# The first mixer group: where its residual comes from

## The chip, the cores and the metric

The kernel runs on one NeuronCore of a Trainium2 chip. It uses TensorE (PE; its weight loads are shown apart as PEld), VectorE (DVE), ScalarE (ACT), GpSimd (POOL) and SyncE (SP), which issues transfers. The metric is the device time of one launch in microseconds (us); lower is better. Times of whole runs are medians; all times inside the kernel come from one profiled execution, counted from the start of its span.

## The reference

Eight batches, eight heads, 576 tokens, head width 64. First an attention with a causal mask and a bias from a running sum, then a mixer: a low-rank product along the sequence (rank 32) and an MLP along the channels, both with a residual. The heads side by side make the 512 features of `x`.

```python
def _attn_ref(q, k, v, s):
    ...
    scores = scale * np.matmul(q, k.transpose(0, 1, 3, 2))
    cum = np.cumsum(np.maximum(s, 0.0), axis=-1)
    bias = -(cum[:, :, :, None] - cum[:, :, None, :])
    scores = np.where(causal, -1000000000.0, scores + np.minimum(bias, 0.0))
    ...
    return np.matmul(attn, v).astype(np.float32)

def _moe_ref(x, U, V, w_ch1, w_ch2):
    xt = x.transpose(0, 2, 1)
    h = xt @ U @ V
    u = x + h.transpose(0, 2, 1)
    ch = np.maximum(u @ w_ch1, 0.0) @ w_ch2
    return (u + ch).astype(np.float32)
```

`U` is 576x32, `V` 32x576, `w_ch1` 512x2048, `w_ch2` 2048x512. What matters below is the last line: the result is the sum of `u` and of the second channel product, and `u` itself is `x` plus the sequence mixer's part.

## The kernel before, in words

**Stages.** The attention works on pairs of heads (32 pairs, four to a batch): `transposes(n)` turns q and k on PE and copies them into a `slot` (lines 303, 323, 326), `scores(n)` makes scores and exponentials (lines 391, 409, 421, 427), `values(n)` multiplies by V (line 455), and DVE divides (line 465) into `x_sb`, a tile of `[token in tile, pair, token tile, feature]`, that is, `x` in token order. `x_sb` is allocated once to a batch from a ring of two.

**The mixer's groups.** The 4608 tokens (8 x 576) are cut into nine groups of 512. A group's `uT` holds `u` with features on the partitions, as the first channel product needs it. For batch 0, `mix_first` makes it: it multiplies `x_sb` by `U_sb` into `ux_first` (line 572; `U_sb` has 128 columns of which 32 are not zero, so rows 32 to 127 of `ux_first` are zero), turns `x_sb` on PE and adds `ux_first` times `V_sb` into the same PSUM tile (lines 579, 587). `mix_first_end` does the last 64 tokens (lines 602, 610). Group 0 is the first 512 tokens of batch 0.

**The channel MLP of a group** is `chanmix(g)`. `hidden` (line 624) makes 16 blocks `hT` with a ReLU on ACT (line 992; the first four of group 0 at line 1135). Group 0 then makes its result by `outputs`: for each of four 128-token tiles `i`, 16 matmuls of 512 columns add up in one PSUM tile (line 634). The first halves of tiles 0 and 1 are made ahead. Line 1017 adds the residual on DVE, line 1023 sends 256 KB. Groups 1 to 8 use `outputs_by_quarters` (line 673) instead, a scheme with fewer products.

**The residual** must be in token order. `by_token` (line 979) fetches it with a transposing transfer from `uT` into `u_sd`, issued on SP; groups 0 to 6 share one `u_sd` buffer. SP also issues the row loads of the slots (line 289), the transposing transfers of `x_sb` to `xT` from batch 2 on (line 472) and the outputs.

**Order.** The text's order is woven: `chanmix` and others are generators in a list `fill`, and attention steps are interleaved with `step_fill()` at a pace; each `yield` is one portion. On PE and POOL the text's order is kept to the end of the kernel (`in_program_order`, line 1263). On DVE, ACT and SP it is kept only up to line 1148, the end of the opening; after that the order on these three is chosen at compile time by the framework's scheduler from its estimates. PSUM tiles for all this (`pwork`) come from a ring of four banks. Between the opening and group 0's outputs, lines 1187 and 1188 copy `V_sb`'s 32 rows to partitions 32 to 127 and into `V_end`, which later batches use.

Of the kernel before, what the change touches and what calls it, by code (L numbers as in the profile page):

```python
# [39 lines left out]
def kernel(  # L40
# [12 lines left out]
    nc = tc.nc  # L53
# [15 lines left out]
    NF = FF // 128  # L69
# [14 lines left out]
    def pwork():  # L84
        return ps_w.tile([128, 512], FP32, tag="w", name="pwork")
# [65 lines left out]
    V_sb = consts.tile([128, S], BF16)  # L151
# [116 lines left out]
    uT_of, x_of, xT_of = {}, {}, {}  # L268

    def uT(g):  # L270
        if g not in uT_of:
            uT_of[g] = work.tile([128, 4, 512], BF16, tag="uT", name="uT", bufs=3)
        return uT_of[g]
# [292 lines left out]
    ux_first = work.tile([128, PB, 128], BF16, tag="ux_first", name="ux_first", bufs=1)  # L566
# [29 lines left out]
        yield  # L596

    def mix_first_end():
        x_sb = x_of.pop(0)
        ut = pwork()[:, 0:256].rearrange("p (a b) -> p a b", a=4)  # L600
        for dt in range(4):
            nc.tensor.matmul(
                ut[:, dt, :],
                lhsT=x_sb[:, dt, 4, :],
                rhs=identity[:, :64],
                start=True,
                stop=False,
                skip_group_check=True,
            )
            nc.tensor.matmul(  # L610
                ut[:, dt, :],
                lhsT=ux_first[:, dt, :],
                rhs=V_sb[:, 512:S],
                start=False,
                stop=True,
                skip_group_check=True,
            )
        nc.vector.tensor_copy(uT(1)[:, 0:4, 0:64], ut)
# [3 lines left out]
    def hidden(f1, u, nf, kts):  # L622
        for kt in kts:
            nc.tensor.matmul(  # L624
                f1,
                lhsT=w1_sb[:, kt, ds(nf * 128, 128)],
                rhs=u[:, kt, :],
                start=(kt == 0),
                stop=(kt == 3),
            )  # L630

    def outputs(f2, hT, i, nfs):
        for nf in nfs:
            nc.tensor.matmul(  # L634
                f2,
                lhsT=hT[:, nf, ds(i * 128, 128)],
                rhs=w2_sb[:, nf, :],
                start=(nf == 0),
                stop=(nf == NF - 1),
                skip_group_check=True,  # L640
            )
            if nf % 4 == 3 and nf < nfs[-1]:
                yield
# [9 lines left out]
    def first_sums(hT, one):  # L653
        if one:
            total(A_1, hT[:, :HF, 256:], hT[:, HF:, 256:], ALU.add, 0)
        else:
            total(A_2, A_1, hT[:, :HF, :256], ALU.subtract, 0)
# [313 lines left out]
    def by_token(u, late=False):  # L971
        if late:
            x_sb = work.tile([128, PB, 5, 128], BF16, tag="x_sb", name="x_sb")
            u_sd = x_sb.rearrange("p a b c -> p (a b c)")[:, 0:2048].rearrange(
                "p (a b c) -> p a b c", a=4, b=4
            )
        else:
            u_sd = work.tile([128, 4, 4, 128], BF16, tag="u_sd", name="u_sd", bufs=1)
        nc.sync.dma_start_transpose(
            out=u_sd.rearrange("p a b c -> p (a b) c"), in_=u.rearrange("p a b -> p (a b)")  # L980
        )
        return u_sd

    def chanmix(g, hT=None, done=0):
        u = uT_of.pop(g)
        if g > 0:
            hT = work.tile([128, NF, 512], BF16, tag="hT", name="hT")
            sums = {1: weight_sums, NG - 3: first_weight_sums}.get(g, lambda: iter(()))()
        for nf in range(done, NF):
            f1 = pwork()  # L990
            hidden(f1, u, nf, range(4))
            nc.scalar.activation(hT[:, nf, :], f1, RELU)  # L992
            if g > 0:
                next(sums, None)
            if g > 0 and nf in (12, 14):
                first_sums(hT, nf == 12)
            if nf == (3 if g > 0 else NF - 1):
                u_sd = by_token(u)
            if nf == NF - 1:
                expanded.append(g)  # L1000
            yield
        if g > 0:
            yield from outputs_by_quarters(g, hT, u_sd)
            return
        ahead = {}
        if g == 0:
            for i in range(2):
                ahead[i] = pwork()
                for _ in outputs(ahead[i], hT, i, range(8)):
                    yield  # L1010
                yield
        for i in range(4):
            f2 = ahead[i] if i in ahead else pwork()
            for _ in outputs(f2, hT, i, range(8 if i in ahead else 0, NF)):
                yield
            o_sb = work.tile([128, DM], FP32, tag="o_sb", name="o_sb", bufs=3)
            nc.vector.tensor_tensor(
                o_sb.rearrange("p (a b) -> p a b", a=4),
                f2.rearrange("p (a b) -> p a b", a=4),
                u_sd[:, :, i, :],  # L1020
                op=ALU.add,
            )
            nc.sync.dma_start(out=out_flat[ds(g * 512 + i * 128, 128), :], in_=o_sb)
            yield
# [120 lines left out]
    hidden_first(2)  # L1145
    hidden_first(3)
    mix_first_end()
    in_program_order(tc, traced, [E.DVE, E.Activation, E.SP])
    load_v(1)
# [7 lines left out]
    load(2)  # L1157
    load_v(2)
    fill.append(chanmix(0, first_hT, 4))
    pace[1] = 0  # L1160
    made = {}
# [29 lines left out]
    weave("V4 V4 S7 V5 S7 V5 S7 V6 S7 V6 T8 T8 V7 S8 V7 S8 T9 S8 T9")  # L1191
    weave("S8 S9 M1 S9 M1 S9 M1 M1 S9 M1 F M1")
    fill.append(chanmix(1))
    pace[1] = 11
    for n in range(2 * PB, NP + 2):
        b, hp = divmod(n, PB)
        if hp == 0 and b < B - 1:
            load(b + 1)
        mixing = seqmix(b - 1) if hp == 1 and b > FT else iter(())
        if b == B:  # L1200
            fill_with(3)
            for _ in range(3):
                step(mixing)
                fill_with(2)
        if n > 2 * PB and n + 1 < NP:
            for at, _ in enumerate(transposes(n + 1)):
                step_fill()
                if at == 0:
                    step(mixing)
        if 2 * PB + 1 < n < NP:  # L1210
            for at, _ in enumerate(scores(n, pT_of(n))):
                step_fill()
                if at == 1:
                    step(mixing)
        for _ in mixing:
            fill_with(1)
        if hp == 1 and FT < b < B:
            fill.append(chanmix(b - 1))
            pace[1] = 12 if b < 6 else 10
        if 2 * PB < n <= NP:  # L1220
            run(values(n - 1, pT_of(n - 1)))
        if hp == 0 and 2 <= b < B - 1:
            load_v(b + 1)
# [20 lines left out]
    for g, sets, fills in ((NG - 2, 4, (0, 0, 2, 4, 6, 8, 10, 12, 14, 17, 20, 23, 25, 26)), (NG - 1, 4, (1, 3, 5, 7, 9, 11, 13, 16, 19, 22, 25, 25, 26, 26))):  # L1244
        u = uT_of.pop(g)
        u_sd = by_token(u, True)
        hT = work.tile([128, NF, 512], BF16, tag="hT", name="hT")
# [46 lines left out]
```

## Time and profile before

| | us |
|---|---|
| median of 3 runs | 361.93 (361.89 to 363.06) |
| profiled execution | 360.82 |
| its span | 359.1 |
| granted PE clock | 1.00 |
| DVE busy in the span | 275.0 |
| ACT busy in the span | 212.8 |
| line 634, first and last start | 48.3, 74.2 |
| line 1017 (four adds), first and last start | 58.4, 74.7 |
| u_sd transfers issued on SP (seven), first and last | 30.9, 277.8 |

The span runs from the first to the last instruction of the program; the execution's own time is 1.7 us longer. Busy time of an engine counts its instructions, not its waits. A matmul's row includes the time to drain, which overlaps with the next, so the step from one matmul's start to the next is what it costs in a stream. Some matmul records are missing: 58 of line 634's 64 are there, while all 64 weight loads are.

### The profile page before, as it was taken

How to read it: one execution, taken by the hardware profiler on the slowest of the kernel's cores; microseconds unless marked ns; L12 is line 12 of the kernel's file. 1: busy time of each engine (PE TensorE's matmuls, PEld its weight loads, DVE VectorE, ACT ScalarE, POOL GpSimd, SP SyncE). 2: the span in 40 equal slices, each digit the busy share in tenths (PEclk: the TensorE clock that was granted, in tenths of full speed). 3: DMA queues.
4: the chain of work that ended last, by engine and by line, in shares of the span. 5: the costliest groups of instructions: out<-in, count | busy, mean ns of one | idle time of the engine just before them, and what ended most of it. 6: DMA issues, size and time to landing. Idle time of an engine off the chain costs nothing.

```text
span 359.1 us, 9577 instructions
## 1 busy us (share of the span) xinstructions
PE 348.8 (97%) x3983; PEld 256.5 (71%) x4022; DVE 275.0 (77%) x608; ACT 212.8 (59%) x322; POOL 84.1 (23%) x102
## 2 busy tenths in 40 slices
PE   8999999999999999999999999999899999999996
PEld 4685566666688567876688667876588548888885
DVE  8685777698889758985799568985797779676774
ACT  4786966757760787157833785358742554675710
POOL 8897261714040404040404022000000000000000
PEclk9999999999999999999999999999999999999999
DMA  7999999999998997999996999172033515010022
GB/s 106 156 200 202 160 178 141 164 160 133 107 112 108 158 133 61 72 120 134 109 94 73 126 149 82 50 162 46 0 49 74 130 36 113 29 60 31 30 89 88
DMA packets 158243, 37.94 MB, mean 106 GB/s; under 512 B 142840, under 2 KB 156568, under 8 KB 158200
## 3 DMA queue, kind: packets, MB, share of 16 engines
q0 software_dynamic: 113136, 18.50, 83.2%
q1 hardware_dynamic: 44776, 18.64, 30.4%
q8 instruction: 31, 0.51, 0.6%
q10 hardware_dynamic: 288, 0.20, 0.2%
q14 instruction: 12, 0.10, 0.1%
HBM read 37.25 MB, written 9.70 MB: 131 GB/s over the span
## 4 chain that ended last, share of the span: by engine, by line
PE 78%; DVE 11%; ACT 4%; DMA 3%; issue 3%; DVEq 0%; ACTq 0%; POOLq 0%
PE pwork L624 22%; PE pwork L673 12%; PE quarter L673 10%; PE pscore L391 8%; PE pwork L455 7%; PE parts L903 6%; PE pwork L303 4%; PE pwork L634 3%; DMA xT<-x_sb 2%; DVE uT L509 2%; DVE slot L651 2%; DVE slot L326 2%; ACT pT L409 2%; ACT hT L992 2%; PE pscore L352 1%
## 5 line engine op out<-in xcount | busy, mean ns | idle before, releaser
L624 PE MATMUL pwork<-uT,w_sb 128*128 128x512 bf16 x401 | 105.9, 379 | 2.6 <-ACT hT L992 0.9
L992 ACT ACTIVATE hT<-pwork 128x512 bf16<-128x512 f32 x108 | 65.2, 608 | 38.4 <-PE pwork L624 38.2
L409 ACT ACTIVATE pT<-pscore 128x1024 bf16<-128x1024 f32 x56 | 56.4, 1030 | 48.7 <-PE pscore L391 47.9
L624 PEld LDWEIGHTS <-w_sb 128*128 128x128 bf16 x448 | 38.3, 98 | 35.9 <-issue 1.3
L391 PE MATMUL pscore<-slot 68*128 68x320 bf16 (+1 forms) x500 | 55.4, 246 | 0.6 <-ACT hT L409 0.3
L391 PEld LDWEIGHTS <-slot 68*128 68x128 bf16 x564 | 41.4, 97 | 16.5 <-issue 0.9
L169 POOL DMA_DIRECT2D v_slot<-in_v_dram x40 | 33.9, 865 | 77.0 <-PE pwork L455 66.3
L673 PEld LDWEIGHTS <-hT 128*128 128x128 bf16 x496 | 46.3, 98 | 7.0 <-DVE uT L509 0.5
L335 DVE TENSOR_TENSOR pT<-pT,keep 128x512 bf16<-128x512 bf16 (+1 forms) x81 | 28.6, 354 | 21.8 <-ACT pT L409 15.9
L323 DVE COPY slot<-pwork 64x576 bf16<-64x576 bf16 x76 | 34.4, 453 | 4.6 <-PE pwork L303 3.7
L455 PEld LDWEIGHTS <-pT 128*128 128x128 bf16 x870 | 32.5, 98 | 6.7 <-issue 1.5
L455 PE MATMUL pwork<-v_slot,pT 128*128 128x65 bf16 x870 | 35.9, 193 | 0.5 <-DVE uT L509 0.4
L465 DVE TENSOR_TENSOR x_sb<-pwork,rec 128x320 bf16<-128x320 f32 x64 | 31.2, 489 | 1.4
L421 ACT ACTIVATE pT<-pscore 128x1024 bf16<-128x1024 f32 x29 | 30.3, 1044 | 2.6 <-PE pscore L391 2.4
L673 PE MATMUL pwork<-w_sb,hT 128*128 128x256 bf16 x240 | 30.6, 273 | 0.0
L326 DVE COPY slot<-pwork 64x576 bf16<-64x576 bf16 x30 | 24.1, 802 | 6.7 <-PE pwork L303 6.2
L673 PEld LDWEIGHTS <-slot 128*128 128x128 bf16 x256 | 24.1, 98 | 4.6 <-issue 1.6
L113 POOL DMA_DIRECT2D q_sd<-in_q_dram x6 | 12.6, 2108 | 45.0 <-PE pwork L303 33.7
L464 DVE RECIPROCAL rec<-pwork 128x5 f32<-128x5 f32 x64 | 12.1, 190 | 12.3 <-PE pwork L455 11.9
L673 PE MATMUL pwork<-w_sum,slot 128*128 128x256 bf16 x160 | 20.3, 273 | 0.7 <-DVE o_sb L687 0.7
L303 PEld LDWEIGHTS <-q_sd 72*128 72x128 bf16 x256 | 14.8, 99 | 8.6 <-DMA q_sd<-in_q_dram 1.0
L303 PE MATMUL pwork<-identity,q_sd 72*128 72x72 bf16 x256 | 18.2, 198 | 0.1
(162 smaller groups left out, 537.1 us busy)
## 6 DMA issues: line engine op xcount, KB each, us to landing
out_dram<-o_sb SPq DMA_DIRECT2D x34, 256.0 KB
v_slot<-in_v_dram POOLq DMA_DIRECT2D x32, 128.0 KB, 7.5
w_sb<-in_moe_w_ch_dram POOLq DMA_DIRECT2D x4, 1024.0 KB, 13.6
q_sd<-in_q_dram POOLq DMA_DIRECT2D x5, 576.0 KB, 13.5
k_sd<-in_k_dram POOLq DMA_DIRECT2D x5, 576.0 KB, 21.9
q_sd<-in_q_dram POOLq DMA_DIRECT2D x4, 288.0 KB, 13.0
k_sd<-in_k_dram POOLq DMA_DIRECT2D x4, 288.0 KB, 12.5
q_sd<-in_q_dram POOLq DMA_DIRECT2D x4, 144.0 KB, 4.9
```

The lines of the kernel that those rows point to most:

```text
L169: nc.gpsimd.dma_start(out=vt[:rows_t, t, :, 0:D], in_=v[b, :, ds(t * 128, rows_t), :].rearrange("h p d -> p h d"),)
L303: nc.tensor.transpose(tps[hh][:, c, t2, :], src[:, 2 * hp + hh, ds(t2 * 128, 128)], identity[:TP, :TP],)
L323: copies(n, hh, par)(by_run[:, :, :, par, :], src)
L326: copies(n, hh, par)(in_turn[:, :, :, :, par], src.rearrange("p c t m -> p c m t"))
L391: nc.tensor.matmul(dst, lhsT=slot[0:KA, hh, ds(S + j * 128, 128)], rhs=slot[0:KA, hh, lo:hi], start=True, stop=True,)
L409: nc.scalar.activation(pT[:, hh, 0:1024], near, EXP, scale=scale)
L421: nc.scalar.activation(pT[:, :, 1024:1536], mid.rearrange("p (a b) -> p a b", a=2), EXP, scale=scale)
L455: nc.tensor.matmul(po[:, i, :], lhsT=pT[:, hh, ds(place(j, i), 128)], rhs=vt[:, j, h, :], start=(j == 0), stop=(j == i), skip_group_check= ...
L465: nc.vector.tensor_tensor(x_sb[:, hp, :, ds(hh * D, D)], po[:, :, 0:D], rec.to_broadcast([128, 5, D]), op=ALU.mult,)
L624: nc.tensor.matmul(f1, lhsT=w1_sb[:, kt, ds(nf * 128, 128)], rhs=u[:, kt, :], start=(kt == 0), stop=(kt == 3),)
L673: nc.tensor.matmul(acc[:, i, :], lhsT=a[:, kt, ds(i * 128, 128)], rhs=b[:, kt, :], start=(begin and i == 0 and kt == 0), stop=(kt == HF - ...
L992: nc.scalar.activation(hT[:, nf, :], f1, RELU)
```

## The change

Group 0 no longer fetches `u` back in token order. Its residual is put together from two parts: `x` itself, which is there in token order as `x_sb`, is added by DVE at the end, and the sequence mixer's part is made by one more matmul at the head of each tile's accumulation, `V_sb`'s 128 columns of the tile as weights and `ux_first` (128x512) as the moving operand. So the PSUM tile holds `h` plus the channel product, and the add brings `x`. The transposing transfer of group 0 is not issued. `x_sb` of batch 0 is kept (`x_of[0]` is read, not popped, in `mix_first_end`) until `chanmix(0)` has used it. The other groups are as before, except that group 1 is now the first user of the `u_sd` buffer.

```diff
     def mix_first_end():
-        x_sb = x_of.pop(0)
+        x_sb = x_of[0]
...
     def outputs(f2, hT, i, nfs):
         for nf in nfs:
+            if nf == 0:
+                nc.tensor.matmul(
+                    f2,
+                    lhsT=V_sb[:, ds(i * 128, 128)],
+                    rhs=ux_first.rearrange("p a b -> p (a b)"),
+                    start=True,
+                    stop=False,
+                    skip_group_check=True,
+                )
             nc.tensor.matmul(
                 f2,
                 lhsT=hT[:, nf, ds(i * 128, 128)],
                 rhs=w2_sb[:, nf, :],
-                start=(nf == 0),
+                start=False,
                 stop=(nf == NF - 1),
                 skip_group_check=True,
             )
...
-            if nf == (3 if g > 0 else NF - 1):
+            if g > 0 and nf == 3:
                 u_sd = by_token(u)
...
+        x_sb = x_of.pop(0)
         ahead = {}
-        if g == 0:
-            for i in range(2):
-                ahead[i] = pwork()
-                for _ in outputs(ahead[i], hT, i, range(8)):
-                    yield
+        for i in range(2):
+            ahead[i] = pwork()
+            for _ in outputs(ahead[i], hT, i, range(8)):
                 yield
+            yield
...
                 o_sb.rearrange("p (a b) -> p a b", a=4),
                 f2.rearrange("p (a b) -> p a b", a=4),
-                u_sd[:, :, i, :],
+                x_sb[:, :, i, :],
                 op=ALU.add,
```

The line `if g == 0` that goes away was always true at that place.

## The prediction

> **What bounds the kernel now.** I read the engine totals first, then the list of what TensorE (PE) waited for, then the rows and the order of time around the group that changes. The totals:
>
> ```profile
> span 359.1 us, 9577 instructions
> PE 348.8 (97%) x3983; PEld 256.5 (71%) x4022; DVE 275.0 (77%) x608; ACT 212.8 (59%) x322; POOL 84.1 (23%) x102
> ```
>
> PE has work for 97% of the span, and the chain that ended last lies on it for 78%. All PE waits of over a tenth that the waits view lists add up to 4.9 us, 1.3 of them before the first matmul. So the first question to any edit here is what it adds to PE or takes from it; the second is whether one of the few waits changes. The rows of the first group's last product (line 634) and of its transfer:
>
> ```profile
> L634 PEld LDWEIGHTS <-hT x64: 95/96/102, 48.3 to 74.0; 128*128 128x128 bf16 x64
> L634 PE MATMUL pwork<-w_sb,hT x58: 376/378/383, 48.4 to 74.2; 128*128 128x512 bf16 x58
> ```
>
> and SP's order of time:
>
> ```profile
> 30.95 7.65 SPq L979 DMA_TRANSPOSE u_sd<-uT  x1
> 46.27 12.08 SPq L289 DMA_DIRECT2D slot<-rows_hbm  x6
> ...
> 75.38 0.35 SPq L1023 DMA_DIRECT2D out_dram<-o_sb  x1
> ```
>
> The reader should see three things: the 64 matmuls (58 recorded) run from 48.4 to 74.2 us, woven between attention work; the transfer that goes away was issued at 30.95; SP then had nothing to issue until 46.27. The first add that reads what the transfer brought (line 1017) starts at 58.4. Nobody waits for it: the view of the tile u_sd names no waiter.
>
> **What is added.** Four matmuls, one at the head of each 128-token tile, of the form 128x512 with 128x128 weights, the form of line 634. The 378 ns of a row includes the time to drain, so the price in a stream is read from the chain, where the next matmul starts:
>
> ```profile
> 68.19 0.86 PE pwork L634 x4
> 69.06 0.06 PE pwork L497
> 69.11 0.44 PE pscore L391 x4
> 69.55 0.86 PE pwork L634 x4
> ```
>
> Here 0.86 us for four gives 0.215 us each, and their weight loads of 96 ns run under the matmul before. So 4 x 0.215 = 0.86 us of PE. The trace does not show this operand pair. Lower bound 0.215 each; upper bound a matmul that overlaps with nothing, 0.378 + 0.096 = 0.474, or 1.90 us for four. I take 0.215, because in that chain a stretch of four takes 0.86 to 0.87 also where its first matmul opens a tile (69.55). The granted clock in all stretches is 1.00.
>
> The Trainium skill, "TensorE: Matmul & The Clock Gate", section "Back-to-back issue gap", puts a sustained stream of weight load and matmul at about 131 ns for 512 columns. By that estimate the four would cost 0.52 us; the row says 0.86, and the row is used.
>
> Do all four lengthen the path? The second tile's opening waits:
>
> ```profile
> 51.13 0.81 DVE L326 COPY slot<-pwork 64x576 bf16<-64x576 bf16 x1
> ...
> 51.63 0.10 PEld L634 LDWEIGHTS <-hT 128*128 128x128 bf16 x1
> ...
> 51.99 0.38 PE L634 MATMUL pwork<-w_sb,hT 128*128 128x512 bf16 x1 [0.17 <-DVE slot L326]
> ```
>
> Its weights were loaded at 51.63. Where nothing holds it, the matmul starts 0.03 after (48.32 to 48.35 at the first tile); here it starts at 51.99, so it stood about 0.33 us for its PSUM bank, which VectorE (DVE) frees at 51.95. That DVE chain (four copies of 0.8 us from 48.37 on) depends on transposes which PE had issued before the first tile. The first added matmul, at 48.35, therefore falls into these 0.33 us: it costs 0. Without that cover it costs its 0.215. The other three stand at about 52.0, 63.0 and 69.4, before stretches without such a hold: 3 x 0.215 = 0.65. One small hold follows the last of them (PE 0.16 at 71.80, put down to issue); I count no gain from it.
>
> The new operands are old by then: V_sb's copies end at 35.3, the last write of ux_first starts at 29.04. So the opening product adds no wait of its own; it takes over the bank wait of the matmul that opened the tile before, and queued behind it on PE are the same matmuls as before.
>
> **What is removed.** One transposing transfer of 128x2048 bf16, 0.52 MB. Next to it the loads ran slower: in 32 to 46 us their queue moved 1.80 MB, or 129 GB/s, against 207 GB/s of all queues in 26 to 34. (207 - 129) x 14 us is 1.09 MB, some 5 us of loading. The Trainium skill, "Advanced Engine Details and Errata", section "X-Bar Transpose (TRN2)", says that such transfers are as fast as ordinary ones; by that, 0.52 MB at 207 GB/s would be an estimate of 2.5 us, so this trace shows the dearer case. What are those 5 us worth? The loads behind it come close: the last V piece of batch 1, issued at 34.18, lands 16.9 later, at 51.1, while its product (line 455) began at 50.58; the second half of the channel weights lets POOL go at 55.67, and the first matmul that needs it starts at 55.95. Yet after 48 us PE's list of waits holds no transfer, and the small stop at 51.1 lies ahead of the DVE hold of 51.95 and is swallowed by it. So 0 now. If that cover were gone, at most the 0.33 of 51.99 would be won. On SP itself nothing was queued behind the removed issue until 46.27.
>
> Farther on, the chain of waits holds one transfer for long, but see what stands beside it in DVE's order of time:
>
> ```profile
> 103.04 7.87 DMA xT<-x_sb
> ```
>
> ```profile
> 110.18 0.68 DVE L687 TENSOR_TENSOR o_sb<-U,pwork 128x512 f32<-128x512 f32 x1
> 110.93 0.56 DVE L509 TENSOR_TENSOR uT<-pwork,xT 128x384 bf16<-128x384 f32 x1
> 111.40 0.68 DVE L687 TENSOR_TENSOR o_sb<-o_sb,u_sd 128x512 f32<-128x512 f32 x1
> 112.00 0.62 DVE L509 TENSOR_TENSOR uT<-pwork,xT 128x128 bf16<-128x128 f32 x2
> ```
>
> DVE ends an add at 110.86 and goes on at 110.93: an earlier landing would win 0.07 us, not 7.87. So the freed transfer time is not passed on there either; I count 0.
>
> **What moves.** (1) Four DVE adds (683 to 692 ns each) read x_sb in place of u_sd, same type and size; the nearest rows, the adds of line 687 that read u_sd in a permuted order, take 648 to 693, so bounds are -0.04 and +0.01 us each, none of it on PE's path; 0. (2) x_sb of batch 0 is held from 32 us until the last of these adds, at 75.4. Two buffers turn, and the next owner is batch 2, whose first write (line 465) follows at 77.24, on the same in-order engine and 1.9 us later: 0; were the add late, what is behind it is a 0.49 us multiply that frees a bank of four. (3) u_sd has a single buffer, so the second group's transposing transfer (issued at 75.83) no longer waits for the last add's end at 75.36; its source is finished about 74.2. It can go at most 1.6 us earlier. Behind it on SP stand the next xT transfer (82.34) and two row loads (83.88); PE waits for none of these in that stretch, so 0. If it passes the last output of group 0, that output leaves up to 6.4 us later; its o_sb is one of three, and the next is needed at about 101. (4) uT of the first group is free earlier; its buffer's next owner writes past 100 us: 0.
>
> **Sum.** 360.82 us (the profiled execution: 359.1 of span and 1.7 around it) + 0.65 = 361.47. The runs' median, 361.93, is 1.11 above that execution, so I add the same 0.65 to it: 362.58, rounded to 362.6. The case's own range is 362.1 (openings partly covered, transfers a little better) to 363.0 (the full 0.86 and some displaced copies). What a measurement can tell from no change is 0.3%, or 1.09 us: faster is under 360.84, slower over 363.02.
>
> **Rivals.** A, faster through the transfers: loads land 5 us earlier, the second group's transfer goes earlier, and the holds of PE from 48 to 113 us go with them. Seen holds, from the starts of neighbouring PE rows: 0.33 at 51.99, 0.15 near 51.1, 0.24 at 60.77, 0.16 at 71.80, 0.3 at 95.00, 0.25 at 107.88, 0.5 at 112.34, together 1.93; 0.86 - 1.93 = -1.07, so 360.9, a little less where DVE gains too. For it: three landings that come just in time, and transfer engines over 90% busy until about 220 us. Against it: every one of these holds is released by DVE, ACT or issue, and those are fed by PE. Chance 0.17.
>
> B, slower through another order: only PE and POOL follow the text's order; on DVE, ACT and SP the order past the opening is set at compile time by the scheduler's own estimates, which four matmuls and a missing transfer shift. Its place is the pair of slot copies (line 326, 0.8 us each) that frees a bank and feeds the scores; put one pair behind an add or a mask and PE stands for it: 0.65 + 1.62 = 2.27, so 364.2. It decides where a pair moves behind another instruction and PE has under 1.6 us of other work queued; at 51.99 and 60.77 it has none. For it: PE already stands at both. Against it: the shift is small and the order elsewhere is set by PE, which moves as a whole. Chance 0.27.
>
> C, the openings don't overlap: 4 x 0.474 - 0.215 covered = 1.68, so 363.6. Against it speaks every 0.86 of the chain. Chance 0.06.
>
> The forecast itself gets 0.50. Faster: most of A and a trace of the forecast, 0.15. Within 0.3%: nearly all of the forecast and the rest of A, 0.50. Slower: B, C and the forecast's upper end, 0.35. The range reaches A's 360.9 and B's 364.2: 360.8 to 364.3.
>
> **What would show it.** Right: four new 128x512 rows that write pwork from V_sb and ux_first, their starts 0.215 before the next; line 634's last start about 0.65 later than 74.2, and the shift still 0.65 at the end; loads landing some 5 us earlier near 50 us without PE gaining; six u_sd transfers from uT instead of seven. A is right if the holds at 60.77, 95.00 and 112.34 shrink; B if the slot copies stand in another order and a PE wait of 0.8 or more appears between 48 and 113; C if a gap follows each new row. The prediction fails if the order of DVE or ACT changes far from the edit.

## The result, and the profile after

The changed kernel takes 361.89 us (median of 22 executions, 361.73 to 362.50). The kernel before, timed beside it, takes 363.64 (22 executions, 361.60 to 367.06). The ratio is 0.9958, 95% interval 0.9940 to 0.9975: faster by 0.42%. Ratios here and below leave out executions more than 1.5% over the fastest of their kernel, so they differ a little from the ratio of the medians. The forecast was 0.65 us slower, no change that can be measured.

The two ranges say more than the medians. The fastest of these executions of the kernel before is as fast as the changed kernel's fastest; its others lie up to 5.5 us above it, while the changed kernel's lie within 0.8 us. The profiled execution of the kernel before (360.82) was faster than all 22 of these. And the profiled execution of the changed kernel is longer than it:

```profile
span 360.4 us, 9583 instructions
PE 349.2 (97%) x3987; PEld 256.5 (71%) x4026; DVE 274.5 (76%) x608; ACT 212.8 (59%) x322; POOL 84.1 (23%) x102
```

So a comparison of these two traces shows what the change costs, and hardly anything of its gain. Of the 1.3 us of span, 0.25 is there already ahead of the first product. The product's rows, then what line 643 (line 634 before) has become:

```profile
L635 PEld LDWEIGHTS <-V_sb x4: 97/98/100, 48.6 to 70.5; 128*128 128x128 bf16 x4
L635 PE MATMUL pwork<-ux_first,V_sb x4: 381/382/383, 48.6 to 70.5; 128*128 128x512 bf16 x4
...
L643 PE MATMUL pwork<-w_sb,hT x58: 377/378/383, 48.8 to 75.6; 128*128 128x512 bf16 x58
```

Four new rows of the same form and duration as before. The last start of the group moves from 74.25 to 75.61; the first product starts at 48.60 where the first matmul started at 48.35, so 1.11 us are added between. From about 116 us to the end DVE's and ACT's instructions are 1.2 us later than in the trace before.

What the change takes away shows in the transfer queues between 34 and 46 us. First the kernel before, then the changed kernel (packets, MB, and the summed time of the packets as a share of the 16 engines' time, which is not used below):

```profile
q0 software_dynamic: 3402, 1.41, 100.8%
q1 hardware_dynamic: 2080, 0.52, 45.6%
```

```profile
q0 software_dynamic: 6187, 2.03, 192.3%
```

q0 carries the loads that POOL issues, q1 the transposing transfer of 0.52 MB. Without that transfer beside it, q0 moves 2.03 MB instead of 1.41 in the same 12 us. The last piece of batch 1's V lands at 47.5 (issued at 35.2, 12.3 us) instead of 51.1. What PE waits for from 45 to 125 us in the changed kernel (in all, times, longest, in us):

```profile
PE pwork L455 <- DVE slot L326: 0.6, 1, 0.6
PE pwork L455 <- DVE uT L509: 0.2, 1, 0.2
PE pwork L624 <- DVE x_sb L465: 0.2, 1, 0.2
PE pwork L643 <- issue: 0.2, 1, 0.2
```

No transfer is among the releasers. To see what the change removes, one needs the trace of an ordinary execution of the kernel before.

### The profile page after: what moved, and what is told of

The parts are those of the page before. It is cut to its first block, busy times and chain, and to the rows that moved or that the text cites. A ratio compares the mean times of both kernels' runs of the same rounds, so it can differ in the third digit from the quotient of the medians.

```text
span 360.4 us, 9583 instructions
## 1 busy us (share of the span) xinstructions
PE 349.2 (97%) x3987; PEld 256.5 (71%) x4026; DVE 274.5 (76%) x608; ACT 212.8 (59%) x322; POOL 84.1 (23%) x102
## 4 chain that ended last, share of the span: by engine, by line
PE 78%; DVE 8%; ACT 4%; issue 3%; POOL 3%; DMA 2%; DVEq 0%; ACTq 0%; POOLq 0%
PE pwork L624 22%; PE pwork L682 13%; PE quarter L682 10%; PE pscore L391 9%; PE pwork L455 7%; PE parts L912 6%; PE pwork L303 3%; PE pwork L643 3%; DVE uT L509 3%; DMA v_slot<-in_v_dram 2%; ACT pT L409 2%; ACT hT L1001 2%; DVE slot L660 1%; PE pwork L912 1%; PE pscore L624 1%
```

## The experiments

There are twelve runs in three groups (e1 to e4, e5 to e8, e9 to e12), each group on another chip. Beside each group the kernel before was timed again on the same chip, with medians of 363.44, 364.21 and 363.64 us; ratios are to those runs. A difference between groups is weaker evidence than one within a group. "PE stands" means that it has to wait.

**e1: the kernel before, profiled again.** No edit.

> The kernel before, unchanged, profiled a second time. Theory T (loads that land just in time): group 0's transposing transfer, from 31 to 45 us, takes transfer time from the loads of batch 1's V, the channel weights' second half and batch 2's q and k; in most executions one of them lands late and PE stands for it. The first profiled execution (360.82) was then a lucky one. T expects times spread over 361.6 to 366 and, if this profiled execution is over 362.5, PE waits released by a transfer between 48 and 60 us, as long as what it lost against 360.82. Rival U (the wait of the second group's transfer for the u_sd buffer, and its place on SP): the loss would stand at 75 to 115 us, with waits released by xT, row loads or what hangs on them.

Measured: 363.95 us (362.48 to 366.05), ratio 1.0012 (0.9985 to 1.0039). The profiled execution took 363.52, near the median. PE's longest waits from 45 to 125 us in it, and PE's order of time around the first:

```profile
PE pwork L455 <- DMA v_slot<-in_v_dram: 1.7, 3, 0.7
PE pwork L455 <- DVE uT L509: 0.6, 1, 0.6
PE pwork L303 <- DMA k_sd<-in_k_dram: 0.5, 1, 0.5
```

```profile
51.65 0.28 PE L455 MATMUL pwork<-v_slot,pT 128*128 128x65 bf16 x4 [0.68 <-DMA v_slot<-in_v_dram]
52.64 0.31 PE L455 MATMUL pwork<-v_slot,pT 128*128 128x65 bf16 x5 [0.71 <-DMA v_slot<-in_v_dram]
53.25 0.67 PE L455 MATMUL pwork<-v_slot,pT 128*128 128x65 bf16 x16 [0.30 <-DMA v_slot<-in_v_dram]
```

Here the pieces of batch 1's V arrive one by one while the product that reads them is running, and PE stops for three of them; the last lands at 53.2, 2.1 us later than in the first profile. Batch 2's k stops it again at 61. By 65 us this execution is 2.5 us behind the first one, 2.4 of it since 48 us. So T holds for this execution; U's place, 75 to 115, carries only 0.2 more.

**e2: the changed kernel with the transfer put back, read by nobody.**

```diff
-            if g > 0 and nf == 3:
+            if nf == (3 if g > 0 else NF - 1):
                 u_sd = by_token(u)
```

> The changed kernel, with group 0's transposing transfer issued as before into u_sd, which nobody reads. T expects the spread of the kernel before to come back, on top of the product's 0.65 to 1.3: median 363.5 to 365.5, range over 2 us wide. U expects the changed kernel's time, 361.9 with a range under 1 us, since the residual still comes from x. If neither, the median is between 362.5 and 363.5.

Measured: 364.66 us (363.05 to 366.01), ratio 1.0038 (1.0013 to 1.0063). The residual and the product are the changed kernel's; only the transfer is back, and with it the spread and 2.8 us. The profiled execution, at 366.01 the slowest of the twelve, lost nothing at 51 us, but at 112. PE's longest wait after 45 us, the chain of waits, DVE's order of time, and the stretches 112 to 120 (PE, PEld, DVE, ACT and POOL busy, granted clock, transfer share, GB/s):

```profile
PE pwork L455 <- DVE uT L509: 2.4, 1, 2.4
```

```profile
104.55 9.96 DMA xT<-x_sb
114.53 0.03 DVE uT L509
```

```profile
114.53 0.56 DVE L509 TENSOR_TENSOR uT<-pwork,xT 128x384 bf16<-128x384 f32 x1 [2.16 <-DMA xT<-x_sb]
```

```profile
112.00:116.00 4.00, 1.56 (x20) 1.26 (x19) 1.84 (x5) 0.00 (x0) 0.00 (x0) 1.00 1.58 158
116.00:120.00 4.00, 4.00 (x45) 3.36 (x45) 2.95 (x8) 0.00 (x0) 0.00 (x0) 0.57 0.79 99
```

and the same two stretches of the changed kernel:

```profile
112.00:116.00 4.00, 3.81 (x61) 3.37 (x59) 4.00 (x10) 0.00 (x0) 0.00 (x0) 1.00 0.29 93
116.00:120.00 4.00, 3.95 (x46) 2.78 (x45) 3.94 (x10) 1.74 (x3) 1.92 (x1) 1.00 0.48 126
```

The xT transfer takes 9.96 us instead of the 7.87 of the first profile. DVE stands 2.16 us for it, PE 2.4 us behind DVE, and then the granted clock falls to half for 3.4 us. Against the changed kernel's trace, DVE is 0.15 us late from 40 us on, 2.4 after the stand, and 4.0 from 124 us to the end; the last 1.6 fall into the stretch of half clock (3.4 us at half speed would be an estimate of 1.7).

**e3: the kernel before with group 0's u_sd in the ring of x_sb.** The second argument of `by_token` puts `u_sd` into a buffer of that ring.

```diff
-                u_sd = by_token(u)
+                u_sd = by_token(u, g == 0)
```

> The kernel before, but group 0's u_sd lies in the ring of x_sb, so that the second group's transfer no longer waits for group 0's adds and may go some 1.5 us earlier, and batch 0's x_sb slot is held until the last add, as in the changed kernel. Group 0's transfer stays. T expects the time of the kernel before, ratio 0.998 to 1.002. U expects the gain of the change plus the 0.65 to 1.3 us of the product that is not paid here: ratio about 0.992 to 0.994.

Measured: 363.87 us (362.15 to 368.18), ratio 1.0004 (0.9972 to 1.0035). In the profile the second group's transfer does go earlier, at 73.79 instead of 75.83. U's 0.992 to 0.994 lies outside the interval, so U falls: the held x_sb slot and the freed u_sd buffer are worth nothing that can be seen.

**e4: the kernel before with half of the channel weights loaded later.**

```diff
                 lhsT=hT[:, nf, ds(i * 128, 128)],
-                rhs=w2_sb[:, nf, :],
+                rhs=w2_sb[:, nf % 8, :],
...
     load_v(1)
-    load_w2(1)
...
     load_v(2)
+    load_w2(1)
```

> The kernel before, with the second half of the second channel weights loaded after batch 2's V instead of before batch 2's q and k; group 0's last product uses the first half of the weights in its place (so group 0's result lacks that half), the same instructions otherwise. Loads of batch 2 come some 5 us earlier, batch 1's V is not touched. T, with the loss at the weights or at batch 2's q and k: ratio 0.993 to 0.996, spread under 1.5 us. T, with the loss at batch 1's V (first read at 50.6 us): ratio 0.998 to 1.002 and the same spread as before. U: no change, ratio 0.998 to 1.002.

Measured: 364.12 us (362.08 to 369.10), ratio 1.0007 (0.9978 to 1.0035). Relief behind batch 1's V buys nothing. The profiled execution, 366.35 and so 2.2 us above the median, stands 0.8 us for batch 1's V, 0.8 for a k load at 87 us and 2.7 behind line 509 up to 116, again with the clock at 0.57 from 116 to 120. So the loss is not cured at the channel weights; in this trace, with the whole amount of bytes unchanged, it stands at V, at the k load and near 112.

**e5: the changed kernel without the product** (group 0's result lacks the sequence mixer's part).

```diff
-            if nf == 0:
+            if False:
                 nc.tensor.matmul(
                     f2,
                     lhsT=V_sb[:, ds(i * 128, 128)],
...
-                start=False,
+                start=(nf == 0),
```

> The changed kernel without the four added matmuls (group 0's result lacks the sequence mixer's part); no transfer. It prices the product by itself. By the forecast's term the four cost 0.65 us: 361.9 - 0.65 = 361.25. If the two traces' shift of 1.1 us between 48 and 72 us is the product alone: 360.8. If the product falls into waits that would be there anyway: 361.8. Spread under 1 us in each case, since the transfer is gone.

Measured: 360.62 us (360.58 to 361.23, 6 executions), ratio 0.9904 (0.9868 to 0.9939). The changed kernel's median, from another group, is 1.27 us higher (361.89 - 360.62). The traces agree: from the first start of the group's matmuls to the last (lines 634, 635 and 643) it takes 25.90 us before, 25.88 in e5 and 27.01 in the changed kernel. So the product costs 1.1 to 1.3 us, about twice the forecast's 0.65.

**e6 and e12: the product before the ninth matmul of a tile.**

```diff
-            if nf == 0:
+            if nf == 8:
...
-                    start=True,
+                    start=False,
...
-                start=False,
+                start=(nf == 0),
```

> The changed kernel with the product placed before the ninth of a tile's 16 matmuls instead of before the first. Tiles 0 and 1 then pay for it at about 56 and 59 us and not ahead of batch 1's first V product. If the extra 0.24 us that PE stood at 52 us in the changed kernel (0.70 against 0.49 in all) comes from the product's place, this is 0.1 to 0.3 us faster than the changed kernel, so 361.6 to 361.8. If not, 361.9 or, as the stand at 52 us no longer covers tile 0's product, up to 0.2 slower.

> The kernel of e6 (product before the ninth matmul of a tile), timed beside the changed kernel on the same chip. If e6's 361.56 was the place of the product: 0.2 to 0.5 us under e11 in the medians. If it was the chip or chance: within 0.1 us of e11.

Measured: e6 361.56 us (361.12 to 363.05), ratio 0.9928 (0.9902 to 0.9954). In the third group, beside the changed kernel as e11:

> The changed kernel, unchanged, timed beside the next one on the same chip: 361.8 to 362.1, spread under 1 us, profile without a PE wait released by a transfer after 45 us.

e12 361.26 us (361.19 to 361.82), ratio 0.9938 (0.9911 to 0.9965); e11 361.87 (361.66 to 362.31), ratio 0.9960 (0.9931 to 0.9989). All but one of e12's twelve executions lie below the fastest of e11: 0.61 us, so this version beats both kernels. PE's order of time in the profiled changed kernel and in e12:

```profile
51.04 0.62 PE L455 MATMUL pwork<-v_slot,pT 128*128 128x65 bf16 x15
52.22 0.64 PE L455 MATMUL pwork<-v_slot,pT 128*128 128x65 bf16 x15 [0.56 <-DVE slot L326]
```

```profile
50.48 1.14 PE L455 MATMUL pwork<-v_slot,pT 128*128 128x65 bf16 x30
51.88 1.02 PE L643 MATMUL pwork<-w_sb,hT 128*128 128x512 bf16 x4 [0.27 <-DVE slot L326]
```

With the product ahead of V's product, the second head of that product waits for DVE's slot copy, 0.56 us by the list, and 0.70 counted from when the next matmul of the stream would have started. With the product later, both heads run on (x30) and the next tile's opening stands behind that copy, for 0.27, as it did before the change. From the group's first start to its last it takes 26.53 us in e12 and 26.51 in e6, against 25.88 in e5: here the product costs 0.64 us. The medians say the same across groups (361.26 - 360.62 = 0.64) and 0.94 within one group (e6 against e5), where e6's spread is wider.

**e7 and e10: half of the transfer, early and late.** Both are the changed kernel with two of the four feature blocks transferred, read by nobody: e7 at the old place in the text, e10 behind the third group's uT. e10's edit, then the place of e7's, which writes into u_sd instead of a tile of its own:

```diff
+    def half_by_token(u):
+        idle = work.tile([128, 2, 4, 128], BF16, tag="idle", name="idle", bufs=1)
+        nc.sync.dma_start_transpose(
+            out=idle.rearrange("p a b c -> p (a b) c"),
+            in_=u[:, 0:2, :].rearrange("p a b -> p (a b)"),
+        )
...
                 u_sd = by_token(u)
+                if g == 2:
+                    half_by_token(u)
```

```diff
-            if g > 0 and nf == 3:
-                u_sd = by_token(u)
+            if nf == (3 if g > 0 else NF - 1):
+                u_sd = by_token(u) if g > 0 else half_by_token(u)
```

> The changed kernel with half of group 0's transposing transfer (two of four feature blocks, 0.26 MB) issued at the old place and read by nobody. T, with a backlog that is carried on: about half of what the whole idle transfer cost (2.8 us over the changed kernel's 361.9), so 362.8 to 363.8, and a spread between. If there is a threshold (loads have some slack), under half: 362.0 to 362.6. If the cost is in the issue and not in the bytes: near 364.5.

> The changed kernel with the same half transfer that cost e7 2.8 us, read by nobody, issued behind the third group's uT, at about 113 us, where the transfer engines are half idle. If it is the time and not the transfer that costs: 361.8 to 362.3, spread under 1 us. If a transposing transfer costs wherever it stands: 363.5 or more.

Measured: e7 364.68 us (361.71 to 372.35), ratio 0.9997 (0.9963 to 1.0030); e10 361.79 (361.63 to 362.44), ratio 0.9971 (0.9944 to 0.9998), with e11 at 361.87 beside it. Late, half of the transfer costs nothing. Early, it brings the spread back: two executions of twelve lost nothing, one lost 10 us. So it is the time that costs. How the cost goes with the bytes is not settled. The median is 2.8 us above the changed kernel's, like e2's, but the kernel before is 0.8 us slower in e7's group than in e2's; over the kernel before beside it, e7 is 0.5 us and e2 1.2, and the intervals of the two ratios overlap. Nor did only the bytes change: in the profiles e7's half is issued at 27.95 us where e2's whole is issued at 31.35, and by the trace's landing events it is in flight for 12.0 us where the whole of the kernel before takes 15.0.

**e8 and e9: the second group's transfer left out,** from the changed kernel and from the kernel before (group 1's residual is read from uT without a turn, so its result is wrong). e9's edit; e8's does the same to the changed kernel:

```diff
-                u_sd = by_token(u)
+                u_sd = by_token(u) if g != 1 else u.rearrange("p a (b c) -> p a b c", b=4)
```

> The changed kernel with the second group's transposing transfer left out too (its residual is read from uT without a turn, so group 1's result is wrong); nothing takes its place. It asks whether the backlog still costs anything in the changed kernel. PE's stands at 52.2, 61.7, 96.4 and 113.5 us there are released by DVE and ACT, not by a transfer, so T expects no change over 0.3 us: 361.6 to 361.9. If the xT landing near 112 still binds, 361.2 to 361.5.

> The kernel before, with the second group's transposing transfer (issued near 76 us) left out: that group reads its residual from uT without a turn, so its result is wrong. Group 0's transfer stays at 31 us. It relieves the transfer engines only after 76 us. Theory T1 (most of the loss stands near 112 us: batch 3's k lands late, batch 4's q leaves 0.3 us after it, xT lands behind them): the loss goes, median 361.9 to 362.6 where the kernel before has its usual 363.4 to 364.2; what remains is the loss at 51 to 61 us. Theory T2 (most of the loss stands at 51 to 61 us, where the loads of batch 1's V and batch 2's k land late): nothing changes, ratio 0.998 to 1.002.

Measured: e8 362.06 us (361.69 to 362.41), ratio 0.9942 (0.9921 to 0.9963), the changed kernel's time: nothing is left to win there. e9 361.48 us (360.63 to 363.17), ratio 0.9957 (0.9928 to 0.9987), against 363.64 for the kernel before beside it. In e9 the transfer at 31 us is still there, and PE still stands for V in the profiled execution, but hardly behind line 509:

```profile
PE pwork L455 <- DMA v_slot<-in_v_dram: 0.5, 1, 0.5
PE pwork L455 <- DVE uT L509: 0.2, 1, 0.2
```

So the medians speak for T1: of the 3.0 us by which the kernel before is usually over the 360.6 that e5 and the fastest of its own executions reach, relief after 76 us takes away 2.2 (1.6 by the ratio); 0.9 is left, with a range of 2.5 us, and its profile puts a stand at V there. e8 is the control: where group 0's transfer is gone, leaving out the second one is worth nothing. One trace points the other way: e1, the only profile of the kernel before that lies near its median, lost 2.4 of its 2.7 us between 48 and 65. The loss has both places; how an ordinary execution divides it is not shown.

## Why the prediction was wrong

**The step that failed** is "So 0 now": the worth of the freed transfer time was put at nothing. It was read from one execution, and that execution lay at the floor of the distribution. Without the transfer and the product (e5) the kernel takes 360.62, which is 3.0 us under the kernel before's 363.64 and 3.6 under its time beside e5; the product takes 1.27 of that back. That these two lead to the measured 361.89 is no check, since both are taken from e5. The check is e2: with the transfer alone put back it takes 364.66, and less the product's 1.27 that is 363.39, where the kernel before took 363.44 beside it. The forecast had 0 and 0.65 for the two terms.

**The baseline.** Three runs from 361.89 to 363.06 and a profile at 360.82 already showed 2.2 us of spread in a kernel whose changed form spreads by 0.8. I carried the 1.11 us between profile and median along as a constant instead of asking where in the kernel an ordinary execution loses it. The median of three was a lucky draw as well: 361.93, where 22 executions give 363.64. That 361.89 lies inside the forecast's range is luck too: a base 1.7 us too low stands against a gain of 3.0 us that was left out.

**The landings.** The prediction listed three landings "that come just in time" and then argued from the list of waits that none of them costs. A list of waits shows what was late in that execution, and here not even all of it: within V's product PE goes from 50.98 to 51.16 for one small matmul where its neighbours take 0.03, and the last piece of V lands at 51.11. So by its time the 0.15 near 51.1 among the forecast's holds is itself a wait for a transfer, too short for the list, and not, as was argued against rival A, released by DVE, ACT or issue. A load of 12 to 17 us that lands at the moment it is read has no slack. In e1 the last piece came 2.1 us later, and V's pieces cost 1.7.

**The xT transfer.** "An earlier landing would win 0.07 us" was right for that trace and asked in one direction only. The 7.87 us of flight (from issue to landing) filled its cover up to 0.07, so a longer flight costs PE about what it is longer. The flights in the profiled executions: 7.1 and 7.9 in the changed kernel, 7.9, 8.1 and 9.0 with the transfer (the first profile, e1, e3), 10.0 to 10.5 in e2, e4 and e7. PE's wait behind line 509 goes with them: 0.2 and 0.4, then 0.4, 0.6 and 1.5, then 2.4 to 3.0, and after these last the half clock. What flies beside it is seen: in e2, e4 and e7 batch 4's k was still landing at 112.5 to 112.9, in the changed kernel it had landed at 105.8. In all of these traces batch 4's q left 0.3 us after batch 3's k had landed (82.5 after 82.2 in the changed kernel, 86.7 after 86.4 in e2, 87.6 after 87.3 in e7). This is a way in which a delay at 34 to 46 us can get to 112; it is read from the times, the views name other releasers for q, and no run tests it. Nor is it the whole story: in e11, without group 0's transfer, batch 3's k lands as late as in e1 (85.4), and PE's wait near 112 is 0.4.

**The product.** The price in the stream was right: the first product's successor starts 0.22 us after it, and no gap follows the other openings, so rival C is out. That the first one would fall into the stand of 0.33 at 52 us was wrong. The stand moved to the second head of V's product and grew (0.15 + 0.33 before, 0.70 now). In both traces it ends with the same pair of slot copies on DVE; that the tiles fell to other banks of the four is inferred, since the views name no banks. e12 takes that back and lands near the forecast's 0.65, though its first product starts only at 55.8, so whatever covers one of the four there is not the stand at 52.

**The rivals.** A named the right cause (loads that come earlier) and one of the right places (the stand near 112), but its price of -1.07 was bounded by the waits of that one trace. B is out: from the opening on, DVE and ACT run the same instructions in the same order in both traces. "What moves" was right at 0 (e3, 1.0004), though the second group's transfer went 2.0 us earlier there, where at most 1.6 had been worked out. The loads did come earlier, by 3.6 us at V where 5 were worked out, and by 0.7 at 76 us.

**What stays open:** why one execution is delayed and another is not, how the cost goes with the bytes, and whether an ordinary transfer of the same bytes at the same time would cost as much as a transposing one; no run has one. That 2.2 of the 3.0 us stand near 112 is worked out from e9's medians and seen in single profiles; of the other executions only the time and the mean clock are on record.

## What to carry to other kernels

Before an edit to transfers is called free, time the kernel often enough to see its spread, and profile an execution near the median: in a kernel whose loads are just in time, the luckiest trace shows hardly any of the waits that the others pay. For each landing, ask what a later one would cost as well as what an earlier one would win. A small product on the busiest engine (0.6 to 1.3 us here) can be cheaper than a transfer that looks hidden, and here its place in the order decided about half of its price.

## What the hardware showed beyond that

A stand of PE of 2.4 to 3.0 us near 113 was followed by 3.41 us of granted clock 0.5 (e2, e4, e7); a stand of 1.5 us in e3 was not. It adds some 1.6 us to the loss in e2. The mean clock of each execution shows how often this happens: it is 0.995 in 28 of the 111 executions of the kernel before that were timed with the experiments, and never below 0.998 in the 88 without group 0's early transfer or in e9's 12. So the half clock is not the main part of an ordinary loss: the other executions timed beside the three groups still have medians of 363.0 to 363.65. The Trainium skill, "TensorE: Matmul & The Clock Gate", section "What's actually happening", gives a free-running activity window of 3413 ns and puts the fall after at least one idle window of about that length; the length of the slow stretch agrees, but here a stand clearly shorter than 3.4 us was enough.
